# Moving q's turn behind the turn of the sums, with GpSimd's two sums beside it, in a fused hash attention and MLP kernel

## The chip, the cores and the metric

The kernel runs on one core of a Trainium2 chip. The metric is the device time of one execution in microseconds (us). The kernel before was timed three times: 871.89, 871.67 and 870.31 us, so a median of 871.67. A profile of one further execution is what the views are read from; its own time is given below.

## The reference, cut to what matters

Hash attention over 4 batches of 8 heads, 768 tokens, head size 64, and behind it a two-layer MLP with a PReLU between, all in float32:

```python
q_bits = (einsum('bhsd,dk->bhsk', q, proj) > 0)          # 6 hash bits per token
k_bits = (einsum('bhsd,dk->bhsk', k, proj) > 0)
mask = q_bucket[:, :, :, None] == k_bucket[:, :, None, :]
scores = where(mask, matmul(q, k^T) / sqrt(64), -1e9)
attn = softmax(scores); attn_out = matmul(attn, v)
x = attn_out as (3072 tokens, 512)
h = x @ w_in                                             # 512 x 2048
g = maximum(h, 0) + alpha * minimum(h, 0)
out = g @ w_out                                          # 2048 x 512
```

## The kernel before, in words

The first part of the kernel is attention, the second (from 318 us on) the MLP, whose products are formed by Strassen-like schemes of seven instead of eight block products. The change lies in the first part.

**Pairs.** Attention goes over 16 pairs of heads (`pi` = 0 to 15), one loop iteration each. TensorE does for a pair, in this order: 12 score cells (`scores`, L782; each two bf16 matmuls on hash bits and four float32 matmuls), the hash projections of the next pair (`hash_bits`, L732), the products with v (`attend`, L815), and the sums over keys (`totals`, L828). The score cells, hash projections and totals share a ring of three double banks of PSUM (`two_banks`). A pair thus goes round: cell 2 of a pair takes the slot that the hash projection had, cell 3 the slot of the sums of the pair before, cell 4 the slot of cell 1.

**ScalarE** forms the exponential of every cell (L785), the sign of the hash projections (L736), the scaling of q (L1230), squares for a check of magnitude (L719), and the first steps of a conversion of MLP weights (`weight_abs`, L604 and L608). One 128 x 512 piece of weights is converted in each half of a pair; the working tiles wx and wr have two buffers, so a piece's first step waits until the piece two before it has been finished on VectorE (L648).

**VectorE** in a pair, in order: the turn of the sums of the pair before (L842), their reciprocals (L843, L845), `vs` (L847), the turn of k for the next pair (`turn_blocks`, L712), a clamp and a shift of weights (L614, L620), the first of five additions over exponentials (L793), the spread of the reciprocals (L854, which needs `rr` from GpSimd), the division (L860), in pairs 8, 10, 12 and 14 a sum of x (`sum_x`, L885), weight steps (L645, L648, L614), the other additions (L801, L797, L798, L804; `totals` needs the last), weight steps (L620, L645, L648), and then the turn of q for the pair after the next (L712).

**GpSimd** forms sums of finished groups of w_in (L667, 16 in all, four per group of four pieces), copies `rr` between partitions (L851, L852), and issues the loads of raw weights (L590) and most of the small transfers that spread the hash bits (L743). A sum is handed out by `weight_sums`, which first copies one element of a VectorE result into `late_sum` (L684), so that GpSimd starts only behind that result. It is called twice in a pair, each time for one sum: in `divide` behind `vs`, ahead of the copies of `rr`, and at the end of the pair behind the last weight step. Behind the fourth sum of a group comes its store, four transfers of 448 KB (L672).

**Queues.** Instructions that go through `do(...)` keep the order of the program on their engine. Transfers that do not go through it are placed by a planner, which may move them on their queue. SyncE's queue (SP) carries the loads of q, k and v, the stores of x and of the sums, and the loads of the second part that are made early (`load_x`, `load_w`, both kept in order for the first batch).

Of the kernel before, what the change touches and what calls it, by code (L numbers as in the profile page):

```python
# [407 lines left out]
def fast_path(  # L408
# [12 lines left out]
    nc = tc.nc  # L421
    P = 128
    B, H, S, D = q.shape
# [62 lines left out]
    def load(pi, name):  # L486
        b, hp = pairs[pi]
        src = {"q": q, "k": k, "v": v}[name]
        if name == "v":
            t = pool.tile([P, 2, NC * D], F32, name=f"vn{pi}", tag="vn")  # L490
            nc.sync.dma_start(t, src[b, 2 * hp : 2 * hp + 2].rearrange("h (p c) d -> p h (c d)", c=NC))
            nat[name, pi] = t
        elif pi and name in BY_BLOCKS:
            load_blocks(pi, name)
        else:
            load_part(pi, name, slice(0, NC), nc.sync)
# [102 lines left out]
    def weight_abs(i, engine=None):  # L599
        i = order[i]  # L600
        lo, hi = halves(i)
        wx[i] = pool.tile([P, 512], F32, name=f"wx{i}", tag="wx")
        wr[i] = pool.tile([P, 512], I32, name=f"wr{i}", tag="wr")
        do(ACT.activation(wr[i], lo, AF.Copy, scale=2.0 ** -29))  # L604
        if engine is DVE:
            do(DVE.tensor_scalar(wx[i].bitcast(U32), hi, 0x7FFFFFFF, None, op0=ALU.bitwise_and))
            return
        do(ACT.activation(wx[i], hi.bitcast(F32), AF.Abs))  # L608
# [39 lines left out]
        do(DVE.tensor_tensor(dst.bitcast(I32), x, r, op=ALU.add))  # L648
        return (dst if i < HW else dst[:, 0])[:, :1]

    sums_due = []

    def weight_group(i):

        i = order[i]
        if i >= HW:
            n, m = divmod(i - HW, 2)
            if m == 1:
                nc.sync.dma_start(w_out_r[:, :, n].rearrange("m p d -> p m d"), wst[HW + n])
            return  # L660
        n, m = divmod(i, 4)
        if m < 3:
            return
        w = wst[n]

        def one(to, a, op, c):
            do(POOL.tensor_tensor(w[:, to], w[:, a], w[:, c], op=op))  # L667

        def store():
            c, kk = divmod(n, 2)  # L670
            for ii in range(4):
                nc.sync.dma_start(w_in_s[4 * c + ii][:, :, kk], w[:, :, ii])  # L672


        for x in ((3, 5, 2), (5, 0, 5), (4, 3, 0), (6, 1, 4)):
            sums_due.append((one, (x[0], x[1], ALU.subtract, x[2])))
        sums_due.append((store, ()))

    late_sum = const.tile([P, 1], F32, name="late_sum")

    def weight_sums(count, after=None):

        if sums_due and after is not None:
            do(POOL.tensor_copy(late_sum, after))  # L684
        while sums_due and count:
            fn, x = sums_due.pop(0)
            count -= fn.__name__ == "one"
            fn(*x)


    def two_banks(name):
# [18 lines left out]
    def turn_blocks(pi, name):  # L710
        tr[name, pi] = pool.tile([P, S], F32, name=f"{name}T{pi}", tag=f"{name}T")
        do(DVE.transpose(tr[name, pi], nat[name, pi].rearrange("p w d -> p (w d)")))  # L712
# [13 lines left out]
    def hash_bits(pi):  # L726

        ps = two_banks(f"hs{pi}")[:, 0, :CW]
        for half in range(2):
            for n, name in enumerate("kq"):  # L730
                c = D * n + 32 * half
                do(PE.matmul(  # L732
                    ps[c : c + 32], wh2, tr[name, pi][:, half * CW : (half + 1) * CW], start=True, stop=True,
                ))
        raw = pool.tile([P, CW], BF16, name=f"hr{pi}", tag="hr", bufs=1)
        do(ACT.activation(raw, ps, AF.Sign, bias=hb2))  # L736
        bits["q", pi], bits["k", pi] = qbs[pi % 2], kb
        for half in range(2):
            for n, name in enumerate("kq"):
                for s in range(2):  # L740
                    c = D * n + 32 * half + NB * s
                    queue = nc.gpsimd if half or name == "q" else nc.scalar
                    queue.dma_start(  # L743
                        bits[name, pi][D * s : D * s + 2 * NB, half * CW : (half + 1) * CW], raw[c : c + 2 * NB],
                    )

    def hash_first(half):

# [83 lines left out]
    def divide(pi, between=lambda: None):  # L832

        b, hp = pairs[pi]
        n = CW // 32
        a = pool.tile([P, CW], F32, name=f"st{pi}", tag="st", bufs=1)
        r = pool.tile([P, n], F32, name=f"rc{pi}", tag="rc")
        rr = pool.tile([P, NCH, n], F32, name=f"rr{pi}", tag="rr")  # L840
        d = pool.tile([P, NCH, CW], F32, name=f"dn{pi}", tag="dn", bufs=1)
        do(DVE.transpose(a, sums[pi][:, 0, :CW]))  # L842
        do(DVE.tensor_scalar(r, a.rearrange("p (n w) -> p n w", w=32)[:, :, 0], S * EPS, None, op0=ALU.add))  # L843
        for g in range(NCH):
            do(DVE.reciprocal(rr[:, g], r))  # L845
        vsum[pi] = pool.tile([P, 1], F32, name=f"vs{pi}", tag="vs")
        do(DVE.tensor_scalar(vsum[pi], av[pi][:, 0, CW : CW + 1], EPS, None, op0=ALU.mult))  # L847
        weight_sums(1, vsum[pi])
        for q0 in (0, D):
            q1 = q0 + 32  # L850
            do(POOL.tensor_copy(rr[q0 : q0 + 32, 1], rr[q1 : q1 + 32, 1]))  # L851
            do(POOL.tensor_copy(rr[q1 : q1 + 32, 0], rr[q0 : q0 + 32, 0]))  # L852
        between()
        do(DVE.transpose(  # L854
            d.rearrange("p g w -> p (g w)"),
            rr.rearrange("p g n -> p (g n)").unsqueeze(2).to_broadcast([P, NCH * n, 32]),
        ))

        x = mid.tile([P, NCH, CW], F32, name=f"x{pi}", tag="x", bufs=1)
        do(DVE.scalar_tensor_tensor(x, av[pi][:, :, :CW], vsum[pi], d, op0=ALU.add, op1=ALU.mult))  # L860
        nc.sync.dma_start(x_s[b, hp], x.rearrange("p g w -> p (g w)"))
# [9 lines left out]
    def load_x(b, *ns):  # L871
        for n in ns or range(4):
            m, kh, ch = ((0, 0, 0), (1, 1, 0), (2, 1, 1), (5, 0, 1))[n]
            t = mid.tile([P, 2, CW], F32, name=f"x{b}_{m}", tag=f"x{m}", bufs=1)
            pinned(b == 0, nc.sync.dma_start(
                t, x_s[b, 2 * kh : 2 * kh + 2].rearrange("k p s -> p k s")[:, :, ch * CW : (ch + 1) * CW],
            ))
            x_m[b, m] = t
# [310 lines left out]

    for pi in range(NPAIR):  # L1190
        i = 2 * pi

        def weight_begin():
            if pi == 1:
                turn_blocks(2, "q")
            if pi + 1 < NPAIR:
                turn_blocks(pi + 1, "k")
            weight_clamp(i)
            weight_parts(i)
            add_first(pi)  # L1200

        if pi:
            scores(pi, CELLS)
            divide(pi - 1, weight_begin)
        else:
            rest = [c for c in CELLS if c not in ahead]
            scores(pi, rest[:4])
            weight_abs(0, DVE)
            scores(pi, rest[4:])
            add_first(pi)  # L1210
            weight_clamp(0)
            weight_parts(0)
        if pi in (8, 10, 12, 14):
            sum_x(0, (8, 10, 12, 14).index(pi), DVE)
        weight_sum(i)
        weight_group(i)
        load_weight(i + 3)
        if pi == 0:
            weight_abs(1, DVE)
        weight_clamp(i + 1)  # L1220
        add_third(pi)
        add_last(pi)
        add_total(pi)
        weight_parts(i + 1)
        weight_sums(1, weight_sum(i + 1))
        weight_group(i + 1)
        load_weight(i + 4)
        if pi + 1 < NPAIR:
            hash_bits(pi + 1)
            do(ACT.activation(tr["q", pi + 1], tr["q", pi + 1], AF.Copy, scale=DOWN))  # L1230
        if 0 < pi < NPAIR - 2:
            turn_blocks(pi + 2, "q")
        attend(pi)
        if pi + 1 == NPAIR:
            now = ff1(0, 0)
            now.step(1)
        totals(pi)
        if pi + 1 == NPAIR:
            now.step(5)
            divide(pi)  # L1240
        else:
            weight_abs(i + 2)
        if pi + 2 < NPAIR:
            load(pi + 2, "v")
        if pi in (9, 11, 15):
            load_w((9, 11, 15).index(pi))
        if pi in (5, 6, 8):
            load_x(0, *{5: (0,), 6: (2, 3), 8: (1,)}[pi])
        if pi == 1:
            setup_alpha()  # L1250
        for name in "qk":
            magnitude(pi, name)
            if pi + 3 < NPAIR:
                load(pi + 3, name)
        if pi + 1 < NPAIR:
            weight_abs(i + 3)


# [95 lines left out]
```

## Time and profile before

| what | us |
|---|---|
| median of three runs | 871.67 (870.31 to 871.89) |
| the profiled execution, its own time | 872.62 |
| its span, first to last instruction | 870.80 |
| TensorE busy | 860.5 |
| VectorE busy | 734.2 |
| ScalarE busy | 375.0 |
| GpSimd busy | 119.1 |

The mean granted clock of TensorE was 0.998. The page says of itself that TensorE's matmuls are pipelined and their ends are modelled; the starts of matmuls are what stalls are read from. In the rows of a timeline the columns are: start, duration, engine, line, operation, output and inputs, shapes, and in brackets the idle time of the engine just before it with what ended it. PE is TensorE, DVE VectorE, ACT ScalarE, POOL GpSimd, SPq SyncE's queue.

### The profile page before, as it was taken

The numbers are of one execution on the slowest core, as the hardware profiler recorded it, in microseconds if no ns is written. First come the engines' busy times: TensorE is split into PE (matmuls) and PEld (weight loads), VectorE is DVE, ScalarE is ACT, GpSimd is POOL, SyncE is SP. The second block draws the span as 40 slices with busy tenths as digits, with TensorE's granted clock in tenths as the row PEclk, the third lists the DMA queues.
The fourth block names the chain that finished last, engine by engine and source line by source line (L and its number), as shares of the span: only waits on it lengthen the run. The fifth ranks groups of instructions, "written<-read, shape, count | busy, mean of one in ns | idle before, by whom it ended". The sixth has DMA issues, their size and how long they took to land.

```text
span 870.8 us, 14641 instructions
## 1 busy us (share of the span) xinstructions
PE 860.5 (99%) x5458; PEld 575.5 (66%) x5458; DVE 734.2 (84%) x1188; ACT 375.0 (43%) x682; POOL 119.1 (14%) x253
## 2 busy tenths in 40 slices
PE   9999999999999999999999999999999999999996
PEld 4444444444445445569985559996558997557996
DVE  6999989999999987899887669897659898568886
ACT  6787878868778733331113331112332112332111
POOL 1322423333435310210000000000000000000001
PEclk9999999999999999999999999999999999999999
DMA  8956796998697446785334335333425433420242
GB/s 197 188 135 130 185 248 176 184 228 207 130 259 177 144 132 236 257 285 222 115 115 121 133 126 165 121 145 92 166 95 163 145 109 115 164 84 1 97 151 72
DMA packets 171104, 135.35 MB, mean 155 GB/s; under 512 B 126240, under 2 KB 155088, under 8 KB 167440
## 3 DMA queue, kind: packets, MB, share of 16 engines
q1 hardware_dynamic: 158528, 108.44, 44.2%
q0 software_dynamic: 9488, 24.56, 9.3%
q10 hardware_dynamic: 3008, 1.33, 0.6%
q8 instruction: 45, 0.74, 0.3%
q14 instruction: 35, 0.29, 0.1%
HBM read 104.87 MB, written 28.31 MB: 153 GB/s over the span
## 4 chain that ended last, share of the span: by engine, by line


## 5 line engine op out<-in xcount | busy, mean ns | idle before, releaser
L782 PE MATMUL sc<-qT,kT 64*128 64x384 f32 x768 | 155.7, 483 | 0.0
L785 ACT ACTIVATE pt<-sc 128x768 f32<-128x768 f32 x192 | 151.5, 811 | 1.2 <-PE sc L782 1.2
L815 PE MATMUL av<-pt,vn 128*32 128x385 f32 (+1 forms) x1536 | 127.0, 485 | 0.0
L815 PEld LDWEIGHTS av<-pt,vn 128*32 128x32 f32 x1536 | 50.3, 109 | 73.8 <-issue 69.8
L782 PEld LDWEIGHTS sc<-qT,kT 64*128 64x128 f32 x768 | 69.2, 187 | 35.0 <-issue 34.0
L975 DVE TENSOR_TENSOR g<-g,g 128x384 f32<-128x384 f32 x128 | 68.3, 554 | 2.2
L1094 POOL DMA_DIRECT2D out_dram<-o x4 | 2.2, 555 | 474.3 <-DVE o L1087 474.3
L782 PE MATMUL sc<-qb,kb 64*128 64x384 bf16 x384 | 65.3, 323 | 1.4 <-ACT pt L785 0.7
L971 DVE SCALAR_TENSOR_TENSOR g<-h,alpha 128x384 f32<-128x384 f32 x60 | 36.8, 614 | 25.2 <-ACT h L964 25.1
L1032 DVE TENSOR_TENSOR ws<-wl 128x512 f32<-128x512 f32 x56 | 38.4, 686 | 21.9 <-DMA wl<-w_out_s 18.0
L1040 DVE TENSOR_TENSOR gs<-g,gs 128x768 f32<-128x768 f32 x56 | 53.3, 952 | 1.0
L1040 DVE TENSOR_TENSOR gs<-g 128x768 f32<-128x768 f32 x56 | 53.2, 950 | 0.0
L782 PEld LDWEIGHTS <-kb 64*128 64x128 bf16 x384 | 21.8, 94 | 36.9 <-issue 13.2
L604 ACT ACTIVATE wr<-raw 128x512 int32<-128x512 uint32 x32 | 22.1, 691 | 35.9 <-DVE wsi L648 18.4
L793 DVE TENSOR_TENSOR accp<-pt,pt 128x1536 f32<-128x1536 f32 x16 | 28.1, 1759 | 8.4 <-ACT pt L785 8.4
L743 POOL DMA_DIRECT2D qb<-hr x60 | 30.1, 507 | 22.8 <-ACT hr L736 22.8
L798 DVE TENSOR_TENSOR accd<-accd,pt 128x1536 f32<-128x1536 f32 x16 | 28.1, 1759 | 1.7
L804 DVE TENSOR_TENSOR accd<-accd,accp 128x1536 f32<-128x1536 f32 x16 | 28.1, 1758 | 0.6
L801 DVE TENSOR_TENSOR accp<-accp,pt 128x1536 f32<-128x1536 f32 x16 | 28.0, 1753 | 0.0
L797 DVE TENSOR_TENSOR accd<-pt,pt 128x1536 f32<-128x1536 f32 x16 | 28.0, 1750 | 0.0
L1230 ACT ACTIVATE qT<-qT 128x768 f32<-128x768 f32 x15 | 12.7, 844 | 26.5 <-DMA kb<-hr 16.4
L915 PE MATMUL f_0a<-x,wi 128*128 128x384 f32 x64 | 23.5, 490 | 0.0
(366 smaller groups left out, 1767.7 us busy)
## 6 DMA issues: line engine op xcount, KB each, us to landing
wi<-w_in_s SPq DMA_DIRECT2D x32, 896.0 KB
wl<-w_out_s SPq DMA_DIRECT2D x16, 1024.0 KB
wl<-w_out_r SPq DMA_DIRECT2D x12, 1024.0 KB
raw<-in_moe_w_in_dram POOLq DMA_DIRECT2D x15, 512.0 KB, 5.2
raw<-in_moe_w_out_dram POOLq DMA_DIRECT2D x14, 512.0 KB, 4.9
w_in_s<-wsi SPq DMA_DIRECT2D x16, 448.0 KB
qn<-in_q_dram SPq DMA_DIRECT2D x64, 96.0 KB
vn<-in_v_dram SPq DMA_DIRECT2D x16, 384.0 KB
```

Of the source, the lines that this page charges most:

```text
L743: queue.dma_start(bits[name, pi][D * s : D * s + 2 * NB, half * CW : (half + 1) * CW], raw[c : c + 2 * NB],)
L782: do(PE.matmul(sc[:, s, :CW], what["k", pi][r, ks], what["q", pi][r, qs], start=first, stop=not first,))
L785: do(ACT.activation(pts[kc][:, g, :, :CW], sc[:, :, :CW], AF.Exp, scale=SCALE / DOWN))
L793: do(DVE.tensor_tensor(accp[pi], p(0), p(1), op=ALU.add))
L797: do(DVE.tensor_tensor(accd[pi], p(3), p(4), op=ALU.add))
L798: do(DVE.tensor_tensor(accd[pi], accd[pi], p(5), op=ALU.add))
L804: do(DVE.tensor_tensor(accd[pi], accd[pi], accp[pi], op=ALU.add))
L815: do(PE.matmul(av[pi][D * s + t : D * s + t + 32, g, :w], nat["v", pi][:, s, kc * D + t : kc * D + t + 32], pts[kc][:, g, s, :w], start=(k ...
L971: do(DVE.scalar_tensor_tensor(new_g(b, m)[:, i], h, al, h, op0=ALU.mult, op1=ALU.max))
L975: do(DVE.tensor_tensor(new_g(b, to)[:, i], g_m[b, x][:, i], g_m[b, y][:, i], op=ALU.subtract))
L1032: do(DVE.tensor_tensor(t, w2[b, n, x], w2[b, n, y], op=op))
L1040: do(DVE.tensor_tensor(t, g2[b, n, x], g2[b, n, y], op=ALU.subtract))
```

## The change

- q of the next pair is turned in `weight_begin`, behind `vs` and ahead of k's turn, in every pair; before, q of the pair after the next was turned at the end of the pair, ahead of the turn of the sums (L842).
- `weight_sums` hands out both of a pair's sums in `divide`; the call at the end of the pair is gone, and with it one copy into `late_sum`. A group's four sums so fall into two pairs following each other.
- The stores of a finished group go into a list. They are issued, in program order, behind v's load at the end of the pair; from pair 14 on at once. v's loads are kept in program order from pair 2 on.
- Of the transfers of hash bits, q's second half comes ahead of k's second half.
- x of the first batch is loaded in pairs 4, 5, 7 and 8, one load each, where it was 5, 6 (two) and 8.
- In pair 1 the second conversion step of weights on ScalarE (`weight_abs(3)`) stands behind the first three score cells; before it stood at the end of pair 0.

```diff
--- before.py
+++ after.py
@@ -488,7 +488,9 @@
         src = {"q": q, "k": k, "v": v}[name]
         if name == "v":
             t = pool.tile([P, 2, NC * D], F32, name=f"vn{pi}", tag="vn")
-            nc.sync.dma_start(t, src[b, 2 * hp : 2 * hp + 2].rearrange("h (p c) d -> p h (c d)", c=NC))
+            ins = nc.sync.dma_start(t, src[b, 2 * hp : 2 * hp + 2].rearrange("h (p c) d -> p h (c d)", c=NC))
+            if pi > 1:
+                do(ins)
             nat[name, pi] = t
         elif pi and name in BY_BLOCKS:
             load_blocks(pi, name)
@@ -648,7 +650,7 @@
         do(DVE.tensor_tensor(dst.bitcast(I32), x, r, op=ALU.add))
         return (dst if i < HW else dst[:, 0])[:, :1]
 
-    sums_due = []
+    sums_due, stores_due = [], []
 
     def weight_group(i):
 
@@ -669,23 +671,27 @@
         def store():
             c, kk = divmod(n, 2)
             for ii in range(4):
-                nc.sync.dma_start(w_in_s[4 * c + ii][:, :, kk], w[:, :, ii])
+                do(nc.sync.dma_start(w_in_s[4 * c + ii][:, :, kk], w[:, :, ii]))
 
 
         for x in ((3, 5, 2), (5, 0, 5), (4, 3, 0), (6, 1, 4)):
             sums_due.append((one, (x[0], x[1], ALU.subtract, x[2])))
-        sums_due.append((store, ()))
+        sums_due.append((stores_due.append, (store,)))
 
     late_sum = const.tile([P, 1], F32, name="late_sum")
+
+    now_stored = []
 
     def weight_sums(count, after=None):
 
         if sums_due and after is not None:
             do(POOL.tensor_copy(late_sum, after))
-        while sums_due and count:
+        while sums_due and (count or sums_due[0][0].__name__ != "one"):
             fn, x = sums_due.pop(0)
             count -= fn.__name__ == "one"
             fn(*x)
+            if now_stored and stores_due:
+                stores_due.pop()()
 
 
     def two_banks(name):
@@ -735,14 +741,12 @@
         raw = pool.tile([P, CW], BF16, name=f"hr{pi}", tag="hr", bufs=1)
         do(ACT.activation(raw, ps, AF.Sign, bias=hb2))
         bits["q", pi], bits["k", pi] = qbs[pi % 2], kb
-        for half in range(2):
-            for n, name in enumerate("kq"):
-                for s in range(2):
-                    c = D * n + 32 * half + NB * s
-                    queue = nc.gpsimd if half or name == "q" else nc.scalar
-                    queue.dma_start(
-                        bits[name, pi][D * s : D * s + 2 * NB, half * CW : (half + 1) * CW], raw[c : c + 2 * NB],
-                    )
+        for name, half, queue in (("k", 0, nc.scalar), ("q", 0, nc.gpsimd), ("q", 1, nc.gpsimd), ("k", 1, nc.gpsimd)):
+            for s in range(2):
+                c = D * "kq".index(name) + 32 * half + NB * s
+                queue.dma_start(
+                    bits[name, pi][D * s : D * s + 2 * NB, half * CW : (half + 1) * CW], raw[c : c + 2 * NB],
+                )
 
     def hash_first(half):
 
@@ -845,7 +849,7 @@
             do(DVE.reciprocal(rr[:, g], r))
         vsum[pi] = pool.tile([P, 1], F32, name=f"vs{pi}", tag="vs")
         do(DVE.tensor_scalar(vsum[pi], av[pi][:, 0, CW : CW + 1], EPS, None, op0=ALU.mult))
-        weight_sums(1, vsum[pi])
+        weight_sums(2, vsum[pi])
         for q0 in (0, D):
             q1 = q0 + 32
             do(POOL.tensor_copy(rr[q0 : q0 + 32, 1], rr[q1 : q1 + 32, 1]))
@@ -1189,17 +1193,23 @@
 
     for pi in range(NPAIR):
         i = 2 * pi
+        if pi == 14:
+            now_stored.append(pi)
 
         def weight_begin():
-            if pi == 1:
-                turn_blocks(2, "q")
             if pi + 1 < NPAIR:
+                turn_blocks(pi + 1, "q")
                 turn_blocks(pi + 1, "k")
             weight_clamp(i)
             weight_parts(i)
             add_first(pi)
 
-        if pi:
+        if pi == 1:
+            scores(1, CELLS[:3])
+            weight_abs(3)
+            scores(1, CELLS[3:])
+            divide(0, weight_begin)
+        elif pi:
             scores(pi, CELLS)
             divide(pi - 1, weight_begin)
         else:
@@ -1222,14 +1232,12 @@
         add_last(pi)
         add_total(pi)
         weight_parts(i + 1)
-        weight_sums(1, weight_sum(i + 1))
+        weight_sum(i + 1)
         weight_group(i + 1)
         load_weight(i + 4)
         if pi + 1 < NPAIR:
             hash_bits(pi + 1)
             do(ACT.activation(tr["q", pi + 1], tr["q", pi + 1], AF.Copy, scale=DOWN))
-        if 0 < pi < NPAIR - 2:
-            turn_blocks(pi + 2, "q")
         attend(pi)
         if pi + 1 == NPAIR:
             now = ff1(0, 0)
@@ -1242,17 +1250,19 @@
             weight_abs(i + 2)
         if pi + 2 < NPAIR:
             load(pi + 2, "v")
+        while stores_due and pi < 14:
+            stores_due.pop(0)()
         if pi in (9, 11, 15):
             load_w((9, 11, 15).index(pi))
-        if pi in (5, 6, 8):
-            load_x(0, *{5: (0,), 6: (2, 3), 8: (1,)}[pi])
+        if pi in (4, 5, 7, 8):
+            load_x(0, {4: 0, 5: 3, 7: 2, 8: 1}[pi])
         if pi == 1:
             setup_alpha()
         for name in "qk":
             magnitude(pi, name)
             if pi + 3 < NPAIR:
                 load(pi + 3, name)
-        if pi + 1 < NPAIR:
+        if 0 < pi < NPAIR - 1:
             weight_abs(i + 3)
```

## Prediction

> **What bounds the kernel now.** I read the page first, then lengths of the attention pairs from the windows view, then the timelines of VectorE, ScalarE and GpSimd at every pair whose length is out of the common. TensorE is busy all the time, so only its stalls can be won or added. A pair's "s" below is its first score matmul; times behind a plus sign are from s.
>
> ```profile
> PE 860.5 (99%) x5458; PEld 575.5 (66%) x5458; DVE 734.2 (84%) x1188; ACT 375.0 (43%) x682; POOL 119.1 (14%) x253
> ```
>
> The windows, cut from s to s (columns: window, its length, PE busy, clock, DMA share, GB/s); pairs 5 to 9:
>
> ```profile
> 105.64:124.71 19.07, 19.04 (x188) 1.00 0.94 230
> 124.71:144.21 19.50, 19.50 (x185) 1.00 0.66 163
> 144.21:163.19 18.98, 18.98 (x189) 1.00 0.99 218
> 163.19:182.17 18.98, 18.98 (x189) 1.00 0.96 236
> 182.17:201.76 19.59, 19.47 (x188) 1.00 0.82 189
> ```
>
> An undisturbed pair is 18.98 us. By the lengths and the distances of score cells, the stalls are: pair 1 0.56, pairs 5 and 6 0.09 + 0.52, pair 9 0.61, pairs 11 and 13 0.39 each, pair 15 0.45: 3.0 us in all. That is nearly all that an edit in this part can win. Pair 9 shows the first gate:
>
> ```profile
> 182.29 0.69 DVE L648 CUSTOM_DVE_ANT_0 wsi<-wx,wr 128x1024 uint16<-128x1024 uint16 x1
> 182.90 0.97 DVE L712 STREAM_TRANSPOSE qT<-qn 128x768 f32<-128x768 f32 x1
> 183.80 0.54 DVE L842 STREAM_TRANSPOSE st<-sm 128x384 f32<-128x384 f32 x1
> ...
> 183.40 0.96 PE L782 MATMUL sc<-qT,kT 64*128 64x384 f32 x4
> 184.39 0.34 PE L782 MATMUL sc<-qb,kb 64*128 64x384 bf16 x2
> ...
> 183.02 0.68 ACT L604 ACTIVATE wr<-raw 128x512 int32<-128x512 uint32 x1 [2.89 <-DVE wsi L648]
> ...
> 184.16 9.33 ACT L785 ACTIVATE pt<-sc 128x768 f32<-128x768 f32 x12
> ```
>
> Cell 3 needs the bank of the sums, which L842 empties; it could have started at +1.63 (183.80) and starts at 184.39. The second gate is ScalarE: its weight conversion (L604) waits for L648, the first exponential follows, and cell 4 needs that one's bank. Call e the end of L648 from s. The exponential starts at e + 1.17 (here +1.99, with e 0.82), on time is +1.03, and 0.55 of lateness is taken up; so this gate costs e - 0.41. Pair 15, with e 0.86 and no q turn, stalls 0.45, as this says.
>
> The last view decides the sign. GpSimd and VectorE hold each other up:
>
> ```profile
> 263.11 0.43 DVE L620 TENSOR_SCALAR wx<-wx 128x512 uint32<-128x512 uint32 x1
> ...
> 263.29 0.30 POOL L851 COPY rr<-rr 32x12 f32<-32x12 f32 x1
> 263.81 1.76 DVE L793 TENSOR_TENSOR accp<-pt,pt 128x1536 f32<-128x1536 f32 x1 [0.27 <-ACT pt L785]
> 263.85 1.77 POOL L851 COPY rr<-rr 32x12 f32<-32x12 f32 x1
> 265.88 0.98 DVE L854 STREAM_TRANSPOSE dn<-rr 128x768 f32<-128x768 f32 x1 [0.32 <-POOL rr L852]
> ...
> 298.73 1.27 POOL L667 TENSOR_TENSOR wsi<-wsi 128x512 f32<-128x512 f32 x1
> 298.98 1.06 DVE L843 TENSOR_SCALAR rc<-st 128x12 f32<-128x12 f32 x1
> ```
>
> A 0.19 us copy lasts 1.77 when it starts 0.04 after the 1.76 add; a 0.17 us tensor_scalar lasts 1.06 when a sum is running, and ends 0.04 after that. Turns (L712) and the clamp L614 run beside sums at their usual 0.97 and 0.64.
>
> **q's turn.** Nothing is added; the 0.90 step of q's turn goes from ahead of L842 to behind L847. L842 then starts at max(+0.15, e): totals end there (0.92 after their start, as at 318.15). Gate one needs e over 1.0 to act again. Left is gate two: pair 9 falls from 0.61 to 0.41, pairs 11 and 13 (e 0.61) from 0.39 to 0.20. Where VectorE is early, it loses some 0.4 that q's turn filled; L620 then ends at +4.13, still ahead of the exponential that lets L793 start at +4.30. That cover is thin: 0.17.
>
> **The sums.** Sixteen remain, now two in each of pairs 4, 5, 7, 8, 10, 11, 13, 14. Before, half of them began ahead of L842, beside q's turn, and half after L847; now both of a pair are queued after L847 (0.37 to the first, 165.25 - 164.88; 1.28 + 0.06 each), and behind them the four copies into rr (0.23 each) for which L854 waits; the raw load (L590) is issued ahead of them, as it was. From L847: the second sum ends at 0.37 + 1.34 + 1.28 = 2.99. L620 began 1.60 after L847 (166.48 - 164.88); with q's 0.90 it is due at 2.50 and cannot finish: bounds are 2.93 (not held) and, by L843's row, some 0.31 after the sum, 3.30; I take 3.30, since L620 itself holds a copy above. L793 follows at 3.33, or at the exponential's +4.30. Rr's first copy gets through as L620 ends, the second is caught by the 1.76 add, as at 263.85, and then two more follow: L854 stands 0.38 + 0.23 = 0.62 late (bounds: nothing, if all copies slip in first; 0.85, if the first is caught too). With L847 at 1.05 after L842, a sum pair that is on time gets L793 at 0.15 + 1.05 + 3.33 = +4.53, which is 0.23 late, and with the 0.62 all later steps are at 5.15 where 4.30 was: 0.85 us.
>
> The Trainium skill, SBUF — State Buffer, section "A bandwidth-pool intuition that's wrong", gives about 115 ns from VectorE's end to the blocked engine's, where the row above has 0.05; by it the 0.62 would be nearer 0.7 and the sum some tenths higher.
>
> **What the delay does to TensorE.** From L793's start a, by pair 9's rows: the last add (L804) ends at a + 12.62 (199.71 - 187.09), L648 at a + 14.42, so the next e is a - 4.56 less the next stalls. Pairs 8, 10, 12, 14 have sum_x, 0.87 more. Totals can't start ahead of that add, and are due at +18.22. In a late pair without sums the exponentials set a = e + 4.10 (1.17, and 187.09 - 184.16); in one with sums a = e + 1.05 + 3.33, and 0.62 on top.
> Pair 4: 5.15, so e is 0.59 in pair 5, stall 0.18. Pair 5: 0.59 + 4.38 + 0.62 = 5.59, e 0.85, stall 0.44 in pair 6, which has no sums and recovers. Pair 7 as 4: 0.18 in pair 8. Pair 8: 5.59 + 13.49 = 19.08 against 18.40, so totals are 0.68 late; behind late totals e is 1.79 - 0.76 = 1.03, stall 0.62 in pair 9, which recovers. Pair 10: 5.15 + 13.49 = 18.64 against 18.22: 0.42, then 0.62 in pair 11. Pair 11: 6.03, 0.44 in pair 12; pair 12 (a 4.95, sum_x) 0.41 in 13; pair 13 0.44 in 14; pair 14 0.68 at totals, 0.62 in 15.
> With pair 1's 0.56 that is 6.3 us of stalls where 3.0 were: +3.3.
>
> **Transfers and ScalarE, taken at nothing beyond pair 6.** Pair 6's 0.61 is hash bits that land late: four stores of sums were issued at 114.10 to 118.98, and the bits at 116.96 to 120.21 behind 1.8 MB. Stores now go out after v's load, over 8 us clear of the next bits; pair 14's go out at some 283, 6 us ahead of its bits, and in pair 8 an overlap cost nothing. So this stall is out of the new sum. On SP's queue the stores (4.3 to 6.1 us per four) now stand ahead of q's and k's loads for three pairs on: k's for pair 8 would be issued by 137.4 and not 132.5, and its turn is at 145.91. x's store waits there too, 5 us of its 18. Were that cover gone, each us over would be a us of VectorE. Pinning v's load holds the queue until attend has ended, as its buffer does now. x's four loads (0.46 to 0.64 each) change pairs only. In the bits, q's second half is issued 1 us sooner and k's 1 us later; k's is first needed by cell 7, at +4.85. Pair 1: two ScalarE rows (1.14) go from ahead of exponential 1 to ahead of exponential 4, which is then as late as before: 0.56 either way.
>
> **Rivals.** (A) Faster: the rows hold nobody up, copies and L620 getting in while L793 waits for its exponential; this decides if L854 is under 0.1 us late in sum pairs. Stalls left are 0.56 + 0.41 + 3 x 0.20 = 1.6, so -1.4 us, 870.2. For it: in five pairs of before (4, 5, 7, 8, 10) a sum ran after L847, and all four copies still started ahead of L793, by 0.03 to 0.17. Against: they now start 1.34 - 0.90 = 0.44 later against VectorE. (B) One copy held (0.38), L620 free: ordinary pairs absorb it (e 0.12), sum_x pairs give 0.58, 0.58, 0.33 and 0.70 behind them; 2.8 in all, -0.3, 871.4: no change. (C) Slower in another way: a load or bits come late behind the stores, 1 to 3 us on top of the forecast; windows of 0.94 to 1.04 DMA share speak for it, the margins above against.
>
> **How the numbers follow.** The sum is against the profiled execution, 872.62 (span 870.80 and 1.82 around it), 0.95 over the median 871.67; I add 3.3 to the median: 875.0. Chances: forecast 0.64, A 0.15, B 0.13, C 0.08. The forecast's own ends, by the same steps: 0.38 for 0.62 gives +1.4, 0.85 gives +5.1. The range goes from just above A, 870.4, to 876.8. What a measurement can tell is 0.2%, 1.74 us: slower is forecast and C, less a little under it; A's -1.4 passes it in about half of its cases: faster 0.08, same 0.23, slower 0.69.
>
> **What would show it.** Right: L854 "<-POOL rr" in eight pairs at 0.4 to 0.9 us, L620 over 0.7 us there, totals waiting for L804 in pairs 8, 10, 14, pair 6 free of its late bits, pairs 9 and 11 over 19.4. Wrong: L620 at 0.43 and L854 without a wait, or pairs 11 and 13 at 19.2 or less; or VectorE's turns waiting for a DMA.

## The result and the profile after

The changed kernel takes 876.13 us in the median of six runs (874.41 to 877.35); the kernel before, on the same chip, 871.54 (870.31 to 872.64). The ratio is 1.0054, with a 95% interval of 1.0040 to 1.0068: slower by 4.6 us. The profiled execution took 875.69 us (span 873.8, mean granted clock 0.997, against 0.998 before); that is only 3.1 above the profiled execution before, which has a wait of 0.9 for a load in its second part (`z_4a` L915 for `wl`) that this one lacks. Lines have moved: the turn of the sums is now L846 (was L842), `vs` L851 (L847), the shift L622 (L620), the first add L797 (L793), the spread L858 (L854), the last weight step L650 (L648), the copies of rr L855 and L856, the turns of q and k L718.

The page's line of busy times of the kernel after:

```profile
PE 860.4 (98%) x5458; PEld 578.2 (66%) x5458; DVE 736.4 (84%) x1188; ACT 372.1 (43%) x682; POOL 121.9 (14%) x241
```

TensorE does the same work (860.5 before), so the loss is in its stalls. VectorE's and GpSimd's busy times rose by 2.2 and 2.8 us with twelve instructions fewer on GpSimd: instructions that lasted longer, not more of them.

The windows of the kernel after, cut from first score matmul to first score matmul (columns: window, its length, TensorE busy, clock, DMA share, GB/s): pairs 5 to 9, then 11 to 14:

```profile
105.42:124.61 19.19, 19.16 (x188) 1.00 0.69 162
124.61:143.84 19.23, 19.16 (x189) 1.00 0.94 231
143.84:163.15 19.31, 19.30 (x188) 1.00 0.80 194
163.15:182.58 19.43, 19.19 (x188) 1.00 0.67 160
182.58:202.02 19.44, 19.16 (x188) 1.00 1.08 272
...
221.51:240.95 19.44, 19.16 (x188) 1.00 0.56 135
240.95:261.17 20.22, 19.23 (x188) 1.00 0.97 258
261.17:281.78 20.61, 19.54 (x186) 1.00 0.76 166
281.78:301.85 20.07, 19.36 (x189) 1.00 0.74 214
```

Less 18.98 each, all pairs stall 7.6 us in sum, where 3.0 were. Two things are to be read apart. Pairs 5, 6, 8, 9, 10, 11 and 15 lose 0.2 to 0.5 each: the delay on VectorE that the prediction worked out. Pair 14's 1.1 is that delay too: 0.45 at cell 4 and 0.63 at the totals, where the forecast had 0.44 and 0.68. Pairs 12 and 13 lose 1.2 and 1.6 where the forecast had 0.44 and 0.41, and pair 7 loses 0.33 where it had nothing: that is something else.

**The delay on VectorE** is there step by step. VectorE and GpSimd in pair 11 of the kernel after:

```profile
223.34 0.10 DVE L851 TENSOR_SCALAR vs<-av 128x1 f32<-128x1 f32 x1
...
225.79 0.83 DVE L622 TENSOR_SCALAR wx<-wx 128x512 uint32<-128x512 uint32 x1
226.54 1.75 DVE L797 TENSOR_TENSOR accp<-pt,pt 128x1536 f32<-128x1536 f32 x1
228.83 0.98 DVE L858 STREAM_TRANSPOSE dn<-rr 128x768 f32<-128x768 f32 x1 [0.54 <-POOL rr L856]
```

```profile
223.71 2.62 POOL L669 TENSOR_TENSOR wsi<-wsi 128x512 f32<-128x512 f32 x2
226.40 0.27 POOL L855 COPY rr<-rr 32x12 f32<-32x12 f32 x1
226.71 1.63 POOL L856 COPY rr<-rr 32x12 f32<-32x12 f32 x1
228.38 0.19 POOL L855 COPY rr<-rr 32x12 f32<-32x12 f32 x1
228.61 0.19 POOL L856 COPY rr<-rr 32x12 f32<-32x12 f32 x1
```

L622 (0.43 when free) starts beside the second sum and ends 0.29 after it (226.62 against 226.33; the forecast had 0.31). One copy slips in, the second is caught by the add and lasts 1.63 instead of 0.19, two more follow, and the spread stands 0.54 late on them. Five of the other seven sum pairs have these rows to within 0.06; in pair 7 the first add came later and caught the third copy instead, and in pair 13 the sums ran during a longer wait.

**The gates** in pair 9, where before cell 3 waited for the sums' bank; the timeline of the kernel after over all engines:

```profile
182.75 0.69 DVE L650 CUSTOM_DVE_ANT_0 wsi<-wx,wr 128x1024 uint16<-128x1024 uint16 x1
...
183.36 0.57 DVE L846 STREAM_TRANSPOSE st<-sm 128x384 f32<-128x384 f32 x1
...
183.47 0.68 ACT L606 ACTIVATE wr<-raw 128x512 int32<-128x512 uint32 x1 [3.75 <-DVE wsi L650]
...
184.61 2.20 ACT L789 ACTIVATE pt<-sc 128x768 f32<-128x768 f32 x3
...
185.46 0.34 PE L786 MATMUL sc<-qb,kb 64*128 64x384 bf16 x2 [0.28 <-ACT pt L789]
```

L846 now follows L650 at once and no cell waits for it. Cell 4 waits for ScalarE, as gate two says: e is 0.86 here (183.44 - 182.58), so 0.45 by e - 0.41, and the pair is 0.46 longer than an undisturbed one.

What TensorE and VectorE waited for in the kernel after (columns: us in all, times, longest):

```profile
PE sm L832 <- DVE accd L808: 2.6, 5, 1.1
PE sc L786 <- ACT pt L789: 1.6, 6, 0.3
...
PE sc L786 <- DMA qb<-hr: 0.8, 1, 0.8
```

```profile
DVE dn L858 <- POOL rr L856: 4.6, 8, 1.0
...
DVE kT L718 <- DMA kn<-in_k_dram: 3.4, 2, 2.8
```

The spread waits for GpSimd in seven of the eight sum pairs (the eighth wait is behind the last pair), and the totals wait for the last add (the five waits are in pairs 0, 8, 10, 13 and 14; those in 8, 10 and 14 were forecast). The two long waits for transfers, of k's turn (2.8) and of a cell (0.8), were not. They follow the third group's stores, which the program places at the end of pair 11; SP's queue in the kernel after:

```profile
244.56 5.91 SPq L674 DMA_DIRECT2D w_in_s<-wsi  x4
250.51 0.69 SPq L895 DMA_DIRECT2D wi<-w_in_s  x1
251.25 1.89 SPq L517 DMA_DIRECT2D qn<-in_q_dram  x2
253.24 9.00 SPq L517 DMA_DIRECT2D kn<-in_k_dram  x4
```

Four loads of k, 96 KB each, take 9.00 us to issue behind the stores. They are for pair 14, and their turn comes in pair 13. VectorE's row there, and TensorE's at both ends of pair 13, in the kernel after:

```profile
266.30 0.98 DVE L718 STREAM_TRANSPOSE kT<-kn 128x768 f32<-128x768 f32 x1 [2.80 <-DMA kn<-in_k_dram]
```

```profile
261.17 0.67 PE L786 MATMUL sc<-qb,kb 64*128 64x384 bf16 x2 [0.82 <-DMA qb<-hr]
...
280.99 0.85 PE L832 MATMUL sm<-accd,ones 128*32 128x384 f32 x8 [1.05 <-DVE accd L808]
```

The turn of k waits 2.80 us, everything on VectorE behind it is late, and at the end of the pair the totals wait 1.05. One pair earlier the small transfers of hash bits, issued from 252.82 to 255.87 among those loads, land late for pair 13's first cell: 0.82. In the kernel before the four stores stood behind k's loads, and neither wait was there; its SP queue:

```profile
245.66 6.12 SPq L515 DMA_DIRECT2D kn<-in_k_dram  x4
251.88 6.14 SPq L672 DMA_DIRECT2D w_in_s<-wsi  x4
```

That the stores' place makes these waits is tested below (`store_last`).

### The profile page after: what moved, and what is told of

It reads as the page before. It is cut to its first block, busy times and chain, and to the rows that moved or that the text cites. A ratio compares the mean times of both kernels' runs of the same rounds, so it can differ in the third digit from the quotient of the medians.

```text
span 873.8 us, 14611 instructions
## 1 busy us (share of the span) xinstructions
PE 860.4 (98%) x5458; PEld 578.2 (66%) x5458; DVE 736.4 (84%) x1188; ACT 372.1 (43%) x682; POOL 121.9 (14%) x241
## 4 chain that ended last, share of the span: by engine, by line
## 5 line engine op out<-in xcount | busy, mean ns | idle before, releaser
L789 ACT ACTIVATE pt<-sc 128x768 f32<-128x768 f32 x192 | 149.3, 814 | 3.9 <-PE sc L786 3.9
L786 PEld LDWEIGHTS <-kb 64*128 64x128 bf16 x384 | 24.1, 94 | 38.5 <-issue 14.6
L797 DVE TENSOR_TENSOR accp<-pt,pt 128x1536 f32<-128x1536 f32 x16 | 28.0, 1753 | 3.8 <-ACT pt L789 3.7
```

The lines of the kernel that those rows point to most:

```text
L786: do(PE.matmul(sc[:, s, :CW], what["k", pi][r, ks], what["q", pi][r, qs], start=first, stop=not first,))
L789: do(ACT.activation(pts[kc][:, g, :, :CW], sc[:, :, :CW], AF.Exp, scale=SCALE / DOWN))
L797: do(DVE.tensor_tensor(accp[pi], p(0), p(1), op=ALU.add))
```

## The experiments

Three theories were set against each other, and the expectations call them by number. Theory 1: GpSimd and VectorE hold each other up, and the delay that the two sums bring to VectorE makes the loss (the forecast's). Theory 2: the moved turn of q is itself the cost. Theory 3: transfers make it, the stores ahead of the loads of q and k. "Against before" is the difference from the median of the kernel before, timed beside it on the same chip.

### First set: the parts one by one

**q's turn alone** (`q_only`), with the store of a group leaving right behind its fourth sum, as the later kernels need:

```diff
-            if pi == 1:
-                turn_blocks(2, "q")
             if pi + 1 < NPAIR:
+                turn_blocks(pi + 1, "q")
                 turn_blocks(pi + 1, "k")
...
-        while sums_due and count:
+        while sums_due and (count or sums_due[0][0].__name__ != "one"):
...
-        if 0 < pi < NPAIR - 2:
-            turn_blocks(pi + 2, "q")
```

> The kernel before with only q's turn moved behind vs; GpSimd's sums are split as before, one of them now starting ahead of the turn of the sums (L842) with nothing but that turn beside it. Theory 1 (GpSimd and VectorE hold each other): the tensor_scalar behind L842 is held by that sum for 0.6 to 0.9 us in the pairs with two sums, as it was once in pair 15 of before; ordinary pairs absorb half of it, so 0 to +1.5 us against before, and no wait of L854 for rr. Theory 2 (the moved turn itself is the cost, because it takes VectorE's slack): +3 us or more, with the tensor_scalar at its 0.17 us. If neither holds, the gates alone give -0.6 us.

Measured 875.44, ratio 1.0056 (1.0035 to 1.0076): 4.1 slower, a miss. SP's queue in this kernel shows why:

```profile
241.83 5.65 SPq L672 DMA_DIRECT2D w_in_s<-wsi  x4
...
254.73 6.70 SPq L515 DMA_DIRECT2D kn<-in_k_dram  x4
```

With the store free to leave earlier, the planner put the third group's four at 241.83, ahead of q's and k's loads. k's turn then waits 2.5 us for its load and a cell 1.8 for hash bits. So this kernel does not tell what q's turn costs: by accident it shows what the stores' place can. The clean test is the next.

**q's turn and nothing else** (`q_turn`): the same without the middle hunk.

> The kernel before with nothing but q's turn moved, and the queue of SyncE in the order of before (in q_only the third group's stores had come to stand ahead of the loads of q and k for pair 14). Theories 1 and 3: pair 13 loses its wait for k's load and its late hash bits, and what stays is the tensor_scalar behind L842, held by the first sum for 0.5 to 0.9 us in the pairs with sums: 2 us or more under q_only, 0 to +2 us against before. If q's turn itself costs, as q_only: +4 us.

Measured 871.94, ratio 1.0003 (0.9994 to 1.0013): no change. The third group's stores stand at 251.25 again, behind k's loads, and all of q_only's 4.1 us but 0.1 are gone: theory 2 falls. What q's turn should win at L842 is lost one instruction later; VectorE in pair 5 of this kernel:

```profile
105.72 0.58 DVE L842 STREAM_TRANSPOSE st<-sm 128x384 f32<-128x384 f32 x1 [0.20 <-PE sm L828]
106.33 0.78 DVE L843 TENSOR_SCALAR rc<-st 128x12 f32<-128x12 f32 x1
```

The sum that before ran beside q's turn now runs beside the turn of the sums and holds L843 behind it (0.17 when free) for 0.78; in the seven other pairs where this happens it lasts 0.57 to 1.08.

**Both sums behind `vs`, q's turn left at the end** (`s_only`):

```diff
-        weight_sums(1, vsum[pi])
+        weight_sums(2, vsum[pi])
...
-        weight_sums(1, weight_sum(i + 1))
+        weight_sum(i + 1)
```

> The kernel before with only the sums moved: both of a pair behind vs, q's turn still at the end of the pair, transfers as before (a group's store may go out as soon as its fourth sum is there). Theory 1: the second sum now ends 2.99 us behind vs while the shift of weights (L620) is due at 1.60, so L620 takes 1.5 to 1.8 us instead of 0.43, and rr's copies are caught by the addition: 1.2 us or more per sum pair, +4 to +6 us against before, more than the whole change. Theory 2 (the moved turn is the cost): within 1 us of before.

Measured 879.94, ratio 1.0095 (1.0080 to 1.0110): 8.6 slower, the right sign and more than expected. VectorE and GpSimd in pair 4 of this kernel:

```profile
90.09 0.43 DVE L620 TENSOR_SCALAR wx<-wx 128x512 uint32<-128x512 uint32 x1
91.14 2.12 DVE L795 TENSOR_TENSOR accp<-pt,pt 128x1536 f32<-128x1536 f32 x1 [0.62 <-ACT pt L787]
94.04 0.98 DVE L856 STREAM_TRANSPOSE dn<-rr 128x768 f32<-128x768 f32 x1 [0.77 <-POOL rr L854]
```

```profile
88.87 2.78 POOL L667 TENSOR_TENSOR wsi<-wsi 128x512 f32<-128x512 f32 x2
91.71 1.61 POOL L853 COPY rr<-rr 32x12 f32<-32x12 f32 x1
```

L620 was expected to be held and was not: without q's turn ahead of it, it starts before the second sum and the sum waits instead. The first add comes next, starts beside the sum, and is held: 2.12 us here, up to 2.50, for its 1.76. The spread follows 0.77 late. And q's turn, still ahead of the turn of the sums, lets gate one act on what is late:

```profile
PE sm L830 <- DVE accd L806: 4.2, 7, 1.1
PE sc L784 <- DVE st L844: 3.0, 7, 0.5
```

**Transfers and small moves alone** (`t_only`): of the change, the list of stores, v's load and the single x loads, the order of the hash bits and pair 1's conversion step; q's turn and the sums as before.

> The kernel before with only the transfers and the two small moves: stores behind v's load, v's load in order, x in single pairs, order of the hash bits, ScalarE's conversion in pair 1. Theory 1: pair 6's 0.6 us goes, nothing else changes, -0.6 to 0 us. Theory 3 (the stores ahead of the loads of q and k make k's late and crowd the hash bits): pair 6's wait comes back in pairs 7 and 13, 0 to +1.5 us, with VectorE's turn of k waiting for a DMA in pair 13.

Measured 873.98, ratio 1.0023 (1.0011 to 1.0036): 2.6 slower. The late bits of pair 6 are gone, as the prediction had it, and the third group's stores, at 243.21 to 249.04, make k's turn in pair 13 wait 1.6. Here nothing about the sums was touched, so these edits lose by themselves, more than the 1.5 that theory 3 expected at most. Not all of the 2.6 is shown to be the stores': by the profile pair 3 starts 0.85 later than in the kernel before, ahead of any store, and the cause of that is not shown.

**q's turn and the sums, without the transfers** (`no_t`): q_only's diff and s_only's together.

> The changed kernel with the transfers and the two small moves undone: q's turn and both sums moved. Theory 1: the larger part of the loss stays, +2.5 to +3.7 us against before; eight waits of L854 for rr of 0.5 to 0.6 us, L620 at 0.83 in the same pairs. Theory 3: a loss of under 1.5 us is left.

Measured 874.16, ratio 1.0028 (1.0017 to 1.0039): 2.8 slower. The shift lasts 0.83 to 0.89 in each sum pair and the spread stands 0.54 late eight times, and no load of k is late. This is the forecast's own mechanism, with only pair 6's late bits, which before has too, beside it. Its third group's stores also stand ahead of k's loads for pair 14 on SP's queue, but 16 us earlier than the changed kernel's:

```profile
228.64 4.57 SPq L672 DMA_DIRECT2D w_in_s<-wsi  x4
```

k's loads follow at 247.75 and are in time. So by these kernels it is not the order alone that costs, but stores right ahead of loads.

### Second set: taking each suspected cost away

**The stores behind q's and k's loads** (`store_last`), all else as changed:

```diff
-        while stores_due and pi < 14:
-            stores_due.pop(0)()
...
         for name in "qk":
             magnitude(pi, name)
             if pi + 3 < NPAIR:
                 load(pi + 3, name)
+        while stores_due and pi < 14:
+            stores_due.pop(0)()
```

> The changed kernel, with the stores of a finished group behind the loads of q and k for three pairs on, and not ahead of them. Theory 3 (the third group's stores make k's load late in pair 13): VectorE's turn of k no longer waits 2.8 us for a DMA there, 1 to 2 us less than the changed kernel (+2.6 to +3.6 us against before); hash bits may come late elsewhere. If the loss of the transfers is not in the queue's order but in the bytes, no change: +4.6 us.

Measured 874.01, ratio 1.0026 (1.0016 to 1.0035): 2.2 slower than before where the changed kernel was 4.6 slower, so 2.4 us are gone; the changed kernel's interval lies above this one. SP's queue in this kernel:

```profile
247.44 6.02 SPq L517 DMA_DIRECT2D kn<-in_k_dram  x4
253.56 6.18 SPq L674 DMA_DIRECT2D w_in_s<-wsi  x4
```

k's turn in pair 13 starts without a wait, no cell waits for hash bits, and pairs 12 and 13 are 19.34 and 19.38 long where they were 20.22 and 20.61. TensorE's waits that are left, for the last add (1.9) and for exponentials (1.8), are the delay's.

**The second sum behind the first add** (`q_s_late`): no_t with one sum behind `vs`, the other behind L793.

```diff
-        weight_sums(2, vsum[pi])
+        weight_sums(1, vsum[pi])
...
             add_first(pi)
+            weight_sums(1, accp[pi][:, 0, :1])
```

> q's turn and the sums moved as in no_t, transfers as before; but the second sum of a pair is handed out behind the first addition (L793), so that it runs beside the spread of the reciprocals and the division, and rr's copies stand ahead of it. Theory 1 (the second sum in front of rr's copies is the cost): L620 is back at 0.43, no wait of L854 for rr in pairs 4 to 14, no totals waiting for L804; 2.5 to 3.5 us less than no_t, so 0 to -1 us against before. Theory 2 (the moved turn is the cost): as no_t, +2.8 us.

Measured 871.79, ratio 0.9998 (0.9988 to 1.0008): the 2.8 us of no_t are gone. GpSimd in pair 8 of this kernel:

```profile
165.03 1.27 POOL L667 TENSOR_TENSOR wsi<-wsi 128x512 f32<-128x512 f32 x1
166.37 0.19 POOL L853 COPY rr<-rr 32x12 f32<-32x12 f32 x1
...
167.05 0.19 POOL L854 COPY rr<-rr 32x12 f32<-32x12 f32 x1
169.66 0.18 POOL L686 COPY late_sum<-accp 128x1 f32<-128x1 f32 x1 [2.42 <-DVE accp L795]
169.80 1.26 POOL L667 TENSOR_TENSOR wsi<-wsi 128x512 f32<-128x512 f32 x1
```

All four copies are through before the add (167.77), the shift lasts 0.43 again, no spread waits in a sum pair, and the second sum runs beside the spread and the division at its usual 1.26. So the loss of no_t was the second sum's place, to within the interval (0.9 us either way).

### Third set: towards a faster version

**best1**: the changed kernel with q_s_late's edit, and a group's four stores split, two at the end of a pair and two at the end of the next.

> The changed kernel with the second sum behind L793 as in q_s_late, and with a group's four store transfers given out two at the end of each of two pairs. Theories 1 and 3 together: both losses go, what is left is pair 1's 0.5 us and ScalarE's gate in pairs 9, 11, 13, 15 at 0.2 to 0.4 us, so -0.5 to -1.5 us against before. If pair 13's wait for k's load stays in spite of the split, +0.5 us.

Measured 872.54, ratio 1.0005 (0.9995 to 1.0015): no gain, a miss. A new wait took the place of the old; VectorE in pair 7 of this kernel:

```profile
154.07 0.69 DVE L650 CUSTOM_DVE_ANT_0 wsi<-wx,wr 128x1024 uint16<-128x1024 uint16 x1 [1.60 <-DMA w_in_s<-wsi]
```

The next group's weights go into the buffer that the second half of the stores, now a pair later, still reads.

**best2**: best1 with VectorE's sums of x in halves over pairs 8 to 15 instead of whole in 8, 10, 12 and 14.

```diff
-        if pi in (8, 10, 12, 14):
-            sum_x(0, (8, 10, 12, 14).index(pi), DVE)
+        if pi >= 8:
+            sum_x(0, (pi - 8) // 2, DVE, pi % 2)
```

> best1 with VectorE's four sums of x in pairs 8, 10, 12, 14 cut into halves, one in each of pairs 8 to 15 (some 0.45 us of VectorE in every pair where it was 0.87 in every second). By the gate e - 0.41, e is then about 0.2 in pairs 9 to 15 and costs nothing: 0.8 to 1.2 us less than best1, -1.5 to -2.5 us against before. If VectorE's load has no part in the stalls that are left, the same as best1.

Measured 872.34, ratio 0.9998 (0.9988 to 1.0008): a miss. The pairs from 9 on are free of stalls in the profile (18.97 to 18.99 each from 9 to 14), which is of the fastest of the twelve executions (870.47); the wait in pair 7 is still there, at 1.8.

**best3**: best2 with only the third group's stores split; the first two groups whole, at the ends of pairs 5 and 8.

```diff
-        for _ in range(2):
+        for _ in range(4 if pi < 9 else 2):
             if stores_due:
                 stores_due.pop(0)()
```

> best2, but with the first two groups' stores given out whole at the end of pairs 5 and 8; only the third group's are split over pairs 11 and 12. In best2 and best1 the split left a group's tile unfree, and VectorE waited 1.6 to 1.8 us for a store in pair 7. Without that wait: 0.8 to 1 us less than best2, so -0.3 to -1.5 us against before by the medians, -2 us by the attention part of the profile.

Measured 869.75 (868.71 to 871.45, eight runs), ratio 0.9975 (0.9963 to 0.9987): 2.1 faster than before, more than expected, and the wait in pair 7 is gone. What is left is bits that land late in pair 13; TensorE in this kernel:

```profile
259.00 0.33 PE L785 MATMUL sc<-qb,kb 64*128 64x384 bf16 x1 [1.03 <-DMA kb<-hr]
```

Why they are late is not shown: best2 has the third group's first two stores at the same place (243.00, here 241.97), and its pair 13 is undisturbed.

**q_late_x**: q_s_late with the sums of x in halves. No transfer is moved in the program, but as in no_t the planner puts the third group's stores early, at 227.83 instead of 251.88.

> q_s_late with VectorE's sums of x in halves over pairs 8 to 15; transfers stay as before, so pair 6 keeps its late hash bits (0.6 to 0.8 us). By the gate e - 0.41 the stalls of pairs 9, 11, 13 and 15 (0.2 to 0.4 us each) go: 0.7 to 1 us less than q_s_late, -0.5 to -1 us against before.

Measured 869.86 (869.24 to 871.96, ten runs), ratio 0.9977 (0.9966 to 0.9989): 2.0 faster than before, more than expected. Pairs 9 to 14 are 18.98 each; pair 6's late bits (0.56) stay. By the profiles the last pair starts 1.5 us earlier than before; the rest of the gain lies in the second part, where the kernel before has its wait of 0.9.

These two beat both kernels and can't be told from each other. q_late_x needs none of the transfers' edits.

### The parts together

| what is in the kernel | us against before |
|---|---|
| q's turn (`q_turn`) | +0.1 |
| both sums behind `vs` (`s_only`) | +8.6 |
| both of these (`no_t`) | +2.8 |
| transfers and small moves (`t_only`) | +2.6 |
| the change | +4.6 |
| the change, stores behind the loads (`store_last`) | +2.2 |
| `no_t`, second sum behind the first add (`q_s_late`) | 0.0 |
| `q_s_late`, sums of x in halves (`q_late_x`) | -2.0 |

q's turn is worth nothing by itself and 5.8 us where both sums stand behind `vs`; the parts don't add. The change's loss is about 2.2 us of held copies and steps (what `store_last` still has, with pair 6's late bits saved), and 2.4 of the stores' place (what it took away).

## Why the prediction was right, and where it was not

The forecast was 875.0, slower by 3.3; measured were 876.13 and 4.6, within the range and of the right sign. That is partly luck: two errors of opposite sign lie under it.

**Right: the sums' mechanism.** L620 taken as held to 3.30 behind `vs`: 3.28. The first add at 3.33: 3.20. The second copy caught, L854 0.62 late: 0.61, counted from its place right behind the add. Waits of the spread in seven of eight sum pairs (0.54, in pair 7 0.32), totals waiting in pairs 8, 10 and 14, pair 6 free of its late bits, pairs 9 and 11 over 19.4: all there. Rivals A and B fall by the rows of L858 and L622; q_s_late, which is A's condition made true (nobody held), shows what A would have been worth without the edits to the transfers: 0.0, not -1.4: pair 6's bits (0.65) still come late, and pair 11 still stalls (0.40) behind pair 10's whole sum of x.

**Right: q's turn.** Gate one is gone from every pair; s_only, which keeps it, pays 3.0 us there. Gate two costs e - 0.41 in the changed kernel and the experiments: 0.45 or 0.46 at e 0.86, 0.21 at e 0.61.

**Mis-sized, too large: the delay's sum.** The forecast put it at 6.3 us of stalls, +3.3; store_last, which keeps the delay and loses the late loads, is at +2.2, and by its pairs' lengths some 5.4 of stalls (an estimate, with the forecast's 0.56 for pair 1). The term that was most too large is e behind late totals: it is 1.79 - 0.94 = 0.85 and not 1.79 - 0.76 = 1.03, since totals start 0.15 after the last add's end, which the forecast left out (220.73 against 220.58 in pair 10). That makes 0.46 where 0.62 stood in pairs 9, 11 and 15. Pair 6 lost 0.25 (0.38 in store_last) where 0.44 stood. VectorE's instructions start some 0.08 ahead of the profiled end of the one before (226.54 against 226.62 for the add, 183.36 against 183.44 for L846), and the forecast had the add start 0.03 after that end. In pair 8 the 0.18 at cell 4 did not come; its totals were 0.64 late in store_last, near the forecast's 0.68, and 0.45 in the changed kernel, where pair 7 had already lost 0.33.

**Wrong: "Transfers and ScalarE, taken at nothing beyond pair 6."** This step failed. The forecast followed the stores through SP's queue for the first group alone and found k's loads there issued by 137.4, with 8 us to spare. In the kernel after they were done at 142.20, as the four stores ahead of them took 7.04 us to issue and the loads themselves 7.51; in the kernel before they took 4.88 and 5.28. For the third group, which the step did not follow, that cover was gone: it also has 0.9 MB for the second part of the kernel on the same queue right behind its stores, k's loads took 9.00, and k's turn waited 2.80. The text named the price ("each us over would be a us of VectorE") and rival C the case (1 to 3 us on top), but gave it 0.08; of the prediction's own signs of being wrong, VectorE's turns waiting for a DMA came true. The runs put the step at 2.4 by store_last. So what happened is C's mechanism on a base 1.1 smaller than the forecast's.

**Partly right: pair 6.** Its 0.61 of late bits is gone, but with the first group's stores now at 124.56 to 131.60, pair 7's first cells lose 0.33. In store_last, where they stand behind k's loads, neither pair has late bits.

## What to carry to other kernels

Where two engines hold each other up, list the steps in the order in which they start: whoever starts first makes the other wait, and short steps that someone waits for (here four copies of 0.19) belong ahead of long ones that nobody waits for (a sum of 1.27). Moving only the second sum behind the first add took all of that loss back. When transfers are moved on a queue, follow every instance of them to the next load behind it and to that load's consumer, not the first instance alone: the four stores cost 0.3 us behind one pair, but behind another most of the 2.4, where a load for a later part of the kernel stood on the same queue. Stores issued some 17 us or more ahead of those loads (no_t, q_s_late, q_late_x) made none late.

## What the runs showed of the hardware

- Who starts first makes the other wait, in both directions. In s_only a first add of 1.76 that starts beside a running sum lasts 2.02 to 2.50, and a sum that starts beside the shift lasts up to 1.43 for its 1.27. The Trainium skill, SBUF — State Buffer, section "SBUF: two separate sides", says the same in words for a VectorE instruction with two SBUF inputs, such as the add, or in a two-port mode: the port pair that VectorE and GpSimd share is held for the whole instruction by whichever starts first. The rows agree on who waits; the turns (0.97) and the accumulating clamp (0.64) ran beside sums at their usual time.
- The one that waits ends a little sooner after the other than its own time, by 0.13 to 0.15 us in these rows: the shift of 0.43 ends 0.29 after the sum and the copy of 0.19 0.05 after the add (changed kernel, pair 11), the add of 1.76 1.61 to 1.62 after the sum (s_only), the tensor_scalar of 0.17 0.04 after it (before, L843). A held step can be priced by that: what is left of the other, plus its own time, less 0.14.
- Four stores of 448 KB from SP's queue took 5.91 to 7.04 us to issue at the ends of pairs 5, 8 and 11 of the changed kernel, and 3.93 to 4.57 in no_t. Four loads of 96 KB right behind them took up to 9.00 us in the changed kernel and 6.02 in store_last, where the stores follow. k's data came some 4 us after the last of those four had been issued (266.30 against 262.24).
- Small transfers on other queues were late at the same place: q's hash bits, issued by 254.88, were not there at 260.35, when the first cell could have started. In store_last, with the stores behind k's loads, no cell waited for them.
